# A four-layer attention kernel: dense outputs in the last layer, spaced background groups, and unread matmuls in thin tiles

## The chip, the core and the metric

The kernel runs on one core of a Trainium2 chip. The metric is the device time of one execution in microseconds (us). Before the change it is 2328.76 us, the median of 3 runs (2326.96 to 2332.97). Engine names in the profile: PE is TensorE's matmuls and PEld its weight loads, DVE is VectorE, ACT is ScalarE, POOL is GpSimd and SP is the engine that issues most transfers. A line such as L1284 is a line of the kernel's source.

## What is computed

Four layers on x of 2048 x 640 in bf16. Each normalizes x, projects it to queries, keys and values for 32 heads of 20, attends, and projects back. Layers 0 and 2 look at a window of 256 keys, layers 1 and 3 at all 2048.

```python
def layer(x, wqkv, wo, window):            # cut and merged from the reference
    h = layernorm(x)                       # no scale, no bias
    q, k, v = split_heads(h @ wqkv)        # 32 heads, 20 wide
    s = einsum("bhqd,bhkd->bhqk", q, k) * 20 ** -0.5
    if window: s = where(0 <= i - j < 256, s, -1e9)
    o = einsum("bhqk,bhkd->bhqd", softmax(s), v)
    return x + merge_heads(o) @ wo

x = layer(x, A_wqkv, A_wo, True)           # layer 0
x = layer(x, B_wqkv, B_wo, False)          # layer 1
x = layer(x, A_wqkv, A_wo, True)           # layer 2
x = layer(x, B_wqkv, B_wo, False)          # layer 3
```

## The kernel before

Work is cut into units: one layer l, one chunk c of 512 queries, one group g of 4 heads. A unit's scores are banks of 128 keys x 512 queries for one head. The main loop goes tile by tile: up to three banks of scores (two buffers, banks 0 to 2 and 3 to 5 of the 8 accumulator banks), one exponential over them on ACT, then the product with the values, two tiles behind. Bank 7 collects that product. All other work (normalizing, projections, outputs, the division by the softmax sum) is *background*: generators that a small scheduler advances between the scores of one tile and those of the next. For these, bank 6 is left, and bank 5 too in the early part of the program ("early"), when every second tile has only two banks.

The scheduler is Python that runs while the program is built, so all of it is fixed in the program. Each tile brings `rate` of credit, and a step of a task costs about its time on TensorE in units of 1 us. A task that yields "hold" is in the middle of an accumulation and goes on whatever the credit is; so a group of matmuls is never split by another task.

```python
def pump(credit, most):
    state["credit"] = min(state["credit"] + credit, most)
    while True:
        t = choose(state["credit"] <= 0.0)     # the held task; else a tail; else, unless blocked, the first of todo
        if t is None: break
        state["credit"] -= advance(t)

def drop_m(b):                                  # a background bank is given back
    mseq[0] += 1
    mfree[b] = (state["tick"] + (not state["early"]), mseq[0])
```

`advance` also counts *heat*: a step's cost divided by 0.22, weighted with 0.15 for tails and 0.7 for the normalization. After the background work of a tile, `keep_clock` adds matmuls that nobody reads until the tile's heat and what was carried over reach `least`, which is 1.76 for a full tile (1.0 early on) and 0 from the units of layer 3 with c > 0 on:

```python
def cool():
    return state["heat"] + state["carry"] < state["least"]

def unread(b):
    nc.tensor.matmul(ps[:, b, :], lhsT=ident[:], rhs=masks[:, 0, :], start=True, stop=True)   # L620
    state["heat"] += 1.0

def keep_clock():
    while cool():
        t = choose(False)
        if t is not None and state["credit"] > -0.5:
            state["credit"] -= advance(t)
            continue
        b = min(mfree, key=mfree.get)
        if mfree[b][0] > state["tick"]:
            break                               # no background bank is free in this tile
        unread(b)
    spare = state["heat"] + state["carry"] - state["least"]
    state["carry"] = min(max(spare, 0.0), 3.0)
    state["heat"] = 0.0
```

Each finished unit starts a *tail* of three steps, which need a background bank each: the softmax sums to a small matrix, its transpose, and the factors spread over the heads; the last line multiplies and stores into `on[:, g, :]`. There the 4 heads of a group lie on partitions 0, 32, 64 and 96, with 20 of each 32 rows used, so the output projection goes over 8 groups of 128 rows:

```python
def t_out(l, c):                                # [...] waits
    for qb in range(4):
        for i in range(2):
            mb = yield from take_m()
            yp = ps[:, mb, 0:HD]
            g0 = G - 2 if last else 0           # last: layer 3, chunk 3; its groups 0 to 5 were done by t_before_last
            for g in range(g0, G):
                nc.tensor.matmul(yp, lhsT=on[:, g, qb * P : (qb + 1) * P],      # L541
                                 rhs=wop[:, g, i * HD : (i + 1) * HD], ...)
                if g < G - 1:
                    yield ("hold", 0.14)
            # [...] add to x on VectorE, give the bank back
            yield ("pe", 0.14)
```

The loop that ties it together:

```python
def rate(t):
    if t >= len(tiles):                         # layer 3, c > 0
        return 0.9
    # [...] 1.2 before layer 1 is woven in; then what the open tasks need, at most 1.0 or 0.9

# for each tile t:
    sp = ps[:, 0:3, :] if t % 2 == 0 else ps[:, 3:7, :]
    # scores: nc.tensor.matmul(sp[:, i, ...], lhsT=u.k(kc, j), rhs=u.q(j, q0, qn), ...)   L1253
    # exponentials: nc.scalar.activation(out=pt[...], in_=sp[...], func=Exp)              L1284
    load_ahead()
    r = rate(t)
    pump(r, r + 0.1)
    keep_clock()
    # values: nc.tensor.matmul(op[32 * j : ...], lhsT=u.v(kc, j), rhs=pg[...], ...)       L1317
```

In layer 3 with c > 0 a tile may take four banks (the last of them bank 6) when no tail and no task is runnable. For the last keys of some units, VectorE computes the exponential instead of ACT (scores at L880, values at L1326).

Of the kernel before, what the change touches and what calls it, by code (L numbers as in the profile page):

```python
# [12 lines left out]
ALU = mybir.AluOpType  # L13
ACT = mybir.ActivationFunctionType

P = 128
# [3 lines left out]
DH = 20  # L20
NT = S // P
KD = D // P
G = 8
C = 512
NC = S // C
EPS = 1e-5
SCALE = DH ** -0.5
HD = D // 2
# [21 lines left out]
def kernel(  # L50
# [75 lines left out]
        nc.sync.dma_start(out=x_sb[:, 4 * c : 4 * c + 4, :], in_=xin[:, 4 * c : 4 * c + 4, :])  # L126
    nc.sync.dma_start(out=wv_sb[1][:], in_=wq_view[1][:, :, 2 * D : 3 * D])

    def load_wop(w):
        v = wo_in[w].rearrange("(g j e) f -> j e g f", g=G, j=4)  # L130
        for j in range(4):
            nc.sync.dma_start(out=wop[32 * j : 32 * j + DH, :, :], in_=v[j])
# [41 lines left out]
    ready = set()  # L174
    todo = []
    tails = []
    state = {"tick": 0, "held": None, "credit": 0.0, "early": True, "act": True, "unit": 0, "heat": 0.0, "carry": 0.0, "least": 0.0}

    class Task:

# [59 lines left out]

    def pump(credit, most):
        state["credit"] = min(state["credit"] + credit, most)
        while True:
            t = choose(state["credit"] <= 0.0)
            if t is None:
                break
            state["credit"] -= advance(t)


    mfree = {5: (0, 0), 6: (0, 1)}  # L250
# [278 lines left out]
    def t_out(l, c):  # L529
        on = ons[l, c]  # L530
        last = (l, c) == (3, NC - 1)
        while last and "before_last" not in ready:
            yield ("wait", 1)
        assert out_seq[out_n[0]] == l % 2
        for qb in range(4):
            for i in range(2):
                mb = yield from take_m()
                yp = ps[:, mb, 0:HD]
                g0 = G - 2 if last else 0
                for g in range(g0, G):  # L540
                    nc.tensor.matmul(  # L541
                        yp, lhsT=on[:, g, qb * P : (qb + 1) * P],
                        rhs=wop[:, g, i * HD : (i + 1) * HD],
                        start=(g == g0), stop=(g == G - 1),
                    )
                    if g < G - 1:
                        yield ("hold", 0.14)
                xv = x_sb[:, 4 * c + qb, i * HD : (i + 1) * HD]
                had = part_o["t"][:, 2 * qb + i, 0:HD] if last else xv
                nc.vector.tensor_tensor(out=xv, in0=had, in1=yp, op=ALU.add)  # L550
                drop_m(mb)
                yield ("pe", 0.14)
            if l < 3:
                stats(l + 1, c, qb)
            else:
                nc.sync.dma_start(out=xout[:, 4 * c + qb, :], in_=x_sb[:, 4 * c + qb, :])
        ons.pop((l, c))
        ready.add(("out", l, c))
        ready.add(("x", l + 1, c))
        n = out_n[0] = out_n[0] + 1  # L560
        if n < len(out_seq) and out_seq[n] != out_seq[n - 1]:
            load_wop(out_seq[n])

    def t_before_last():

        on = ons[3, NC - 1]
        for qb in range(4):
            for i in range(2):
                mb = yield from take_m()
                yp = ps[:, mb, 0:HD]  # L570
                for g in range(G - 2):
                    nc.tensor.matmul(
                        yp, lhsT=on[:, g, qb * P : (qb + 1) * P],
                        rhs=wop[:, g, i * HD : (i + 1) * HD],
                        start=(g == 0), stop=(g == G - 3),
                    )
                    if g < G - 3:
                        yield ("hold", 0.14)
                xv = x_sb[:, 4 * (NC - 1) + qb, i * HD : (i + 1) * HD]
                nc.vector.tensor_tensor(  # L580
                    out=part_o["t"][:, 2 * qb + i, 0:HD], in0=xv, in1=yp, op=ALU.add
                )
                drop_m(mb)
                yield ("pe", 0.14)
        ready.add("before_last")
# [27 lines left out]

    def cool():

        return state["heat"] + state["carry"] < state["least"]

    def unread(b):

        nc.tensor.matmul(  # L620
            ps[:, b, :], lhsT=ident[:], rhs=masks[:, 0, :], start=True, stop=True
        )
        state["heat"] += 1.0
# [8 lines left out]
# [5 lines that stand above are left out]
                state["credit"] -= advance(t)  # L637
                continue
            b = min(mfree, key=mfree.get)
            if mfree[b][0] > state["tick"]:  # L640
                break
            unread(b)
        spare = state["heat"] + state["carry"] - state["least"]
        state["carry"] = min(max(spare, 0.0), 3.0)
        state["heat"] = 0.0
# [360 lines left out]
    def t_tail(l, c, g, on, oT):  # L1006
        def fill(count):

            for n in range(count * ((l, c, g) == (3, NC - 1, G - 1))):
                nc.tensor.matmul(  # L1010
                    ps[:, 0, :], lhsT=ident[:], rhs=masks[:, 0, :], start=True, stop=True
                )

        yield ("wait", 2)
        fill(2)
        mb = yield from take_m()
        warm_bank(mb)
        zp = ps[:, mb, 0:16]
        for qb in range(4):
            nc.tensor.matmul(  # L1020
                zp[:, 4 * qb : 4 * qb + 4], lhsT=oT[:, qb * P : (qb + 1) * P],
                rhs=sel4[:], start=True, stop=True,
            )
        rz = rzp.tile([P, 16], F32, name="rz", tag="rz")
        nc.vector.reciprocal(out=rz[:], in_=zp)  # L1025
        drop_m(mb)

        hl = rzp.tile([P, 2, 16], BF16, name="hl", tag="hl")
        nc.vector.tensor_copy(out=hl[:, 0, :], in_=rz[:])
        nc.vector.tensor_tensor(out=hl[:, 1, :], in0=rz[:], in1=hl[:, 0, :], op=ALU.subtract)  # L1030
        yield ("pe", 0.25)
        fill(3)
        yield ("wait", 2)
        mb = yield from take_m()
        warm_bank(mb)
        rp = ps[0:32, mb, :].bitcast(BF16)[:, 0:P]
        nc.tensor.transpose(out=rp, in_=hl[:].rearrange("p n r -> p (n r)"), identity=ident[:])
        rT = rzp.tile([32, P], BF16, name="rT", tag="rT")
        nc.vector.tensor_copy(out=rT[:], in_=rp)  # L1039
        drop_m(mb)  # L1040
        yield ("pe", 0.1)
        fill(1)
        yield ("wait", 2 if state["tick"] < last_tick[0] else 1)
        mb = yield from take_m()
        warm_bank(mb)
        zb = ps[:, mb, :]
        for qb in range(4):
            nc.tensor.matmul(  # L1048
                zb[:, qb * P : (qb + 1) * P], lhsT=spread4[:, qb, :], rhs=rT[:],
                start=True, stop=True,  # L1050
            )
        nc.vector.tensor_tensor(out=on[:, g, :], in0=oT[:], in1=zb, op=ALU.mult)  # L1052
        drop_m(mb)
        yield ("pe", 0.3)
        fill(3)
        ready.add(("tail", l, c, g))
        if (l, c, g) == (3, NC - 1, G - 3):
            push("before_last", t_before_last(), 0, 8.0)
        if g == G - 1:
            need = first_use(l + 1, c, 0) if l < 3 else len(units) + c  # L1060
            push(("out", l, c), t_out(l, c), need, 9.0)
            if l < 3:
                push_layer(l + 1, c)
    def t_zeros():

        z = ka_all[:, G : G + 4, :].rearrange("p a b -> p (a b)")
        yield ("wait", 4)
        for n in range(2):
            nc.gpsimd.dma_start(
                out=wop[:, 4 * n : 4 * n + 3, :].rearrange("p g f -> p (g f)"), in_=z[:, 0 : 3 * D]  # L1070
            )
            nc.gpsimd.dma_start(out=wop[:, 4 * n + 3, :], in_=z[:, 0:D])
            yield ("wait", 1)
        load_wop(0)
        for t in (*kts, *qts):
            nc.gpsimd.dma_start(out=t[:], in_=z[:, 0 : t.shape[1]])
            yield ("wait", 1)
        ready.add("kts")
# [67 lines left out]
    with tc.manual_schedule():  # L1146
# [49 lines left out]
        def rate(t):  # L1196

            if t >= len(tiles):
                return 0.9
            u = tiles[t][0][0]  # L1200
            if index[u.l, u.c, u.g, u.part] < woven:
                return 1.2
# [16 lines left out]
        while ended is None or t < ended + 8:  # L1219
# [3 lines left out]
            if t < len(tiles) or banks:  # L1223
# [23 lines left out]
                if n_b == 4:  # L1247
                    mseq[0] += 1
                    mfree[6] = (state["tick"] + 2, mseq[0])
                for n in range(2):  # L1250
                    for i, (u, j, m, b0, subs, first, last, end) in enumerate(cur):
                        for kc, q0, qn, col in subs[n : n + 1]:
# [37 lines left out]
                    pts.append((t, pt, i, b))  # L1290
                warmth = 1.76 if state["unit"] >= woven else 1.0
                state["least"] = warmth * n_b / 3 if state["unit"] < index[3, 1, 0, None] else 0.0
                load_ahead()
                r = rate(t)
                pump(r, r + 0.1)
# [98 lines left out]
```

## Time and profile before

| | |
|---|---|
| median of 3 runs | 2328.76 us |
| profiled execution, span | 2334.1 us |
| busy: ACT / PE / DVE | 2177.3 / 2019.9 / 1465.6 us |
| mean granted TensorE clock | 0.852 of full |
| unread matmuls (L620) | 788 |
| output matmuls (L541, and 48 for the first part of the last chunk) | 976 |

The page gives the busy time of each engine and its share of the span, then the span in 40 slices with the busy share in tenths, and the clock that TensorE was granted, also in tenths. The groups that follow it are one line of the source each: the operation, output and input by the program's names, how often, total busy time and mean duration, and the idle time of the engine just before them with what ended it. A wait of one engine for another costs time only if that engine is the one that sets the pace of its stage. So the busy shares have to be read stage by stage.

### The profile page before, as it was taken

The page shows a single profiled execution, that of the slowest core. Times are in us where ns is not written, and L with a number is a line of the kernel's source. Part 1 is how long each engine was busy: PE and PEld are TensorE (multiplying, and loading weights), DVE is VectorE, ACT ScalarE, POOL GpSimd, SP SyncE. Part 2 cuts the span into 40 slices and gives each one's busy share as a digit, 9 for nine tenths or more (in the row PEclk, how much of TensorE's full clock was granted, in tenths as well). Part 3 has the DMA queues.
Part 4 walks back from the last instruction along what each step waited for, and adds up shares of the span by engine and source line. Part 5 has one row for each costly group of instructions (what it writes and reads, how often), then busy time and mean ns, then how long its engine had stood idle before and what let it go on. Part 6 is the DMA issues. An engine that isn't in the chain of part 4 may idle for free.

```text
span 2334.1 us, 40627 instructions
## 1 busy us (share of the span) xinstructions
PE 2019.9 (87%) x15793; PEld 725.3 (31%) x15793; DVE 1465.6 (63%) x2726; ACT 2177.3 (93%) x1751; POOL 273.7 (12%) x445
## 2 busy tenths in 40 slices
PE   8899999988899888888988898898878888888887
PEld 3344333333323332233322333342322122222222
DVE  6677776426646666666666544452677777777772
ACT  6788889999999998999899899999999999999997
POOL 4332321201100012000120013001000000000000
PEclk9999999999989999999999999999855565556556
DMA  6232322322200123102230023112200010011100
GB/s 189 82 88 79 100 75 64 83 64 65 83 19 27 46 69 95 48 14 55 75 103 25 18 84 107 39 27 78 64 29 27 27 38 27 27 38 37 29 14 12
DMA packets 84881, 132.57 MB, mean 57 GB/s; under 512 B 19760, under 2 KB 60080, under 8 KB 84688
## 3 DMA queue, kind: packets, MB, share of 16 engines
q1 hardware_dynamic: 65472, 76.80, 11.9%
q0 software_dynamic: 19216, 53.17, 7.9%
q8 instruction: 124, 2.03, 0.4%
q14 instruction: 69, 0.57, 0.1%
HBM read 98.70 MB, written 27.79 MB: 54 GB/s over the span
## 4 chain that ended last, share of the span: by engine, by line
ACT 41%; PE 28%; issue 14%; DVE 12%; DMA 1%; POOL 0%; SPq 0%; ACTq 0%; DVEq 0%; POOLq 0%
ACT pt L1284 40%; PE ps L1253 7%; PE ps L354 5%; PE ps L541 4%; PE ps L1317 4%; DVE pt L1353 3%; PE ps L455 3%; PE ps L620 2%; DVE st L304 1%; DVE on L1052 1%; ACT ka L1284 1%; DVE raw_o L887 1%; DVE oT L839 1%; PE ps L419 1%; DVE raw_o L897 1%
## 5 line engine op out<-in xcount | busy, mean ns | idle before, releaser
L1284 ACT ACTIVATE pt<-ps 128x1536 bf16<-128x1536 f32 (+2 forms) x1641 | 2100.2, 1502 | 114.8 <-PE ps L1253 107.0
L1253 PE MATMUL ps<-qt,kt 32*128 32x512 bf16 x4008 | 642.1, 456 | 192.8 <-ACT pt L1284 160.9
L1317 PE MATMUL ps<-pt,vt 128*21 128x512 bf16 x3860 | 466.9, 456 | 0.3 <-ACT pt L1284 0.3
L1253 PEld LDWEIGHTS <-kt 32*128 32x128 bf16 x4008 | 190.4, 94 | 610.8 <-issue 589.7
L1353 DVE TENSOR_TENSOR pt<-pt,masks 128x1024 bf16<-128x1024 bf16 (+5 forms) x403 | 238.0, 624 | 127.3 <-ACT pt L1284 126.8
L620 PE MATMUL ps<-masks,ident 128*128 128x512 bf16 x788 | 270.6, 396 | 28.3 <-DVE rT L1039 11.9
L354 PE MATMUL ps<-xnT,wqk 128*128 128x512 bf16 x830 | 220.2, 390 | 14.2 <-DVE on L1052 3.7
L1317 PEld LDWEIGHTS <-vt 128*21 128x21 bf16 x3960 | 100.0, 90 | 319.8 <-issue 310.6
L304 DVE CAST st<-ps 128x512 bf16<-128x512 f32 x128 | 88.4, 690 | 159.9 <-PE ps L354 159.7
L541 PE MATMUL ps<-wop,on 128*128 128x320 bf16 x976 | 167.6, 315 | 5.5 <-DVE x_sb L550 2.3
L1253 PE MATMUL ps<-qa,ka 32*128 32x384 bf16 (+2 forms) x1408 | 117.6, 277 | 30.6 <-ACT pt L1284 25.8
L887 DVE TENSOR_SCALAR xnT<-ps 128x512 int32<-128x512 f32 x88 | 60.8, 690 | 106.6 <-PE ps L880 106.2
L1052 DVE TENSOR_TENSOR on<-oT,ps 128x512 bf16<-128x512 bf16 x128 | 87.3, 682 | 59.9 <-PE ps L1048 57.3
L839 DVE CAST oT<-ps 128x512 bf16<-128x512 f32 x112 | 76.7, 685 | 73.4 <-PE ps L1317 49.1
L550 DVE TENSOR_TENSOR x_sb<-x_sb,ps 128x320 bf16<-128x320 bf16 x120 | 57.9, 482 | 100.3 <-PE ps L541 100.0
L455 PE MATMUL ps<-wv,xnT 128*128 128x320 bf16 x640 | 108.6, 302 | 10.4 <-DVE rz L1025 3.8
L541 PEld LDWEIGHTS <-on 128*128 128x128 bf16 x976 | 90.5, 101 | 71.6 <-issue 37.3
L354 PEld LDWEIGHTS <-wqk 128*128 128x128 bf16 x830 | 71.0, 98 | 110.4 <-issue 52.2
L620 PEld LDWEIGHTS <-ident 128*128 128x128 bf16 x788 | 59.3, 97 | 130.5 <-issue 128.6
L388 POOL TENSOR_SCALAR rstd<-mv 128x4 f32<-128x4 f32 x15 | 4.9, 328 | 794.1 <-DVE mv L375 794.1
L1317 PE MATMUL ps<-pt,va 128*21 128x384 bf16 (+2 forms) x1408 | 79.5, 283 | 6.9 <-DVE pt L1353 5.5
L1253 PEld LDWEIGHTS <-ka 32*128 32x128 bf16 x1408 | 44.3, 92 | 98.2 <-issue 89.8
(107 smaller groups left out, 1794.4 us busy)
## 6 DMA issues: line engine op xcount, KB each, us to landing
vt<-v_d SPq DMA_DIRECT2D x48, 336.0 KB
kt<-k_d SPq DMA_DIRECT2D x192, 80.0 KB
wqk<-in_B_wqkv_dram POOLq DMA_DIRECT2D x80, 160.0 KB, 3.9
wqk<-in_A_wqkv_dram POOLq DMA_DIRECT2D x70, 160.0 KB, 3.5
k_d<-st POOLq DMA_DIRECT2D x75, 128.0 KB, 2.2
q_d<-st POOLq DMA_DIRECT2D x75, 128.0 KB, 2.2
qt<-q_d SPq DMA_DIRECT2D x384, 20.0 KB
v_d<-vs POOLq DMA_DIRECT2D x16, 336.0 KB, 3.1
```

What stands on the lines that cost most here:

```text
L304: nc.vector.tensor_copy(out=out_, in_=in_)
L354: nc.tensor.matmul(pq, lhsT=wt[:, dc, :], rhs=xt[:, dc, :], start=(dc == 0), stop=(dc == KD - 1),)
L455: nc.tensor.matmul(pv, lhsT=xt[:, dc, i * P : (i + 1) * P], rhs=wv_sb[l % 2][:, dc, h * HD : (h + 1) * HD], start=(dc == 0), stop=(dc == K ...
L541: nc.tensor.matmul(yp, lhsT=on[:, g, qb * P : (qb + 1) * P], rhs=wop[:, g, i * HD : (i + 1) * HD], start=(g == g0), stop=(g == G - 1),)
L620: nc.tensor.matmul(ps[:, b, :], lhsT=ident[:], rhs=masks[:, 0, :], start=True, stop=True)
L839: nc.vector.tensor_copy(out=oT[:], in_=op)
L887: V.tensor_scalar(out=xi.bitcast(I32)[:, i * C : (i + 1) * C], in0=side["psum"], scalar1=SCALE * LOG2E * E23, scalar2=127.0 * E23, op0=ALU ...
L1052: nc.vector.tensor_tensor(out=on[:, g, :], in0=oT[:], in1=zb, op=ALU.mult)
L1253: nc.tensor.matmul(sp[:, i, col * P : (col + qn) * P], lhsT=u.k(kc, j), rhs=u.q(j, q0, qn), start=True, stop=True,)
L1284: nc.scalar.activation(out=pt[:, i:k, b0 * P :], in_=sp[:, i:k, b0 * P :], func=ACT.Exp, scale=SCALE,)
L1317: nc.tensor.matmul(op[32 * j : 32 * j + VW, q0 * P : (q0 + qn) * P], lhsT=u.v(kc, j), rhs=pg[:, i, col * P : (col + qn) * P], start=(first ...
L1353: nc.vector.tensor_tensor(out=pt_[:, i:k, b0 * P :], in0=pt_[:, i:k, b0 * P :], in1=mv_, op=ALU.mult,)
```

## The change

Three things are changed together.

*Spacing.* After the first step of a background task in a tile, a further task starts only when the credit left is over 0.6. Held tasks and tails are not affected.

*Dense outputs of the final layer.* In layer 3, a tail stores its group into a staging slot (5, 6 or 7 of `on`), and small transfers move each head's 20 rows to their place in 640 dense rows: five blocks of 128. The output weights are loaded in the same order, so a group of the projection takes 5 matmuls in place of 8. The last two groups of the last chunk keep the old layout; the first part of that chunk takes 4 in place of 6. The credit in layer 3 with c > 0 falls from 0.9 to 0.45 a tile.

*Unread matmuls in poor tiles.* From the units of layer 1 with c > 0 until `least` is 0, a tile counts as cool, too, while its own heat is under 0.9. Where no background bank is free, `keep_clock` no longer stops: it owes the matmul, and what is owed is issued into the first score bank of the next tile, ahead of its scores, which overwrite it.

```diff
 def pump(credit, most):
     state["credit"] = min(state["credit"] + credit, most)
+    floor = 0.0
     while True:
-        t = choose(state["credit"] <= 0.0)
+        t = choose(state["credit"] <= floor)
         if t is None:
             break
         state["credit"] -= advance(t)
+        if t not in tails:
+            floor = 0.6
```

```diff
+    def packed(l, c):
+        return l > 2
 # t_out
+        dense = packed(l, c) and not last
+        a, b = (0, KD) if dense else (G - 2 if last else 0, G)
-                for g in range(g0, G):
+                for g in range(a, b):
 # t_before_last (first part of the last chunk)
-                for g in range(G - 2):
+                for b in range(4):
+                    n = min(P, (G - 2) * 80 - b * P)
 # [...] operands on[0:n, b, ...] and wop[0:n, b, ...]
 # t_tail
-        nc.vector.tensor_tensor(out=on[:, g, :], in0=oT[:], in1=zb, op=ALU.mult)
+        end = (l, c) == (3, NC - 1) and g >= G - 2
+        spread = packed(l, c) and not end
+        nu = on[:, 5 + g % 3 if spread else g, :]
+        nc.vector.tensor_tensor(out=nu, in0=oT[:], in1=zb, op=ALU.mult)
 # [...]
+        if spread:
+            yield ("wait", 2)
+            for j in range(4):
+                r, a = (4 * g + j) * DH, 0
+                while a < DH:
+                    b, o = divmod(r + a, P)
+                    n = min(DH - a, P - o)
+                    nc.sync.dma_start(
+                        out=on[o : o + n, b, :], in_=nu[32 * j + a : 32 * j + a + n, :]
+                    )
+                    a += n
+            if g == G - 1 or (l, c, g) == (3, NC - 1, G - 3):
+                yield ("wait", 3)
 # rate
-                return 0.9
+                return 0.45
 # [...] load_wop(w, dense): the weights in dense order for layer 3, and the old order of the last two groups beside them
```

```diff
 def cool():
+        if state["least"] > 0.0 and state["heat"] < state["floor"]:
+            return True
         return state["heat"] + state["carry"] < state["least"]
 # keep_clock
             b = min(mfree, key=mfree.get)
-            if mfree[b][0] > state["tick"]:
+            if state["early"] and mfree[b][0] > state["tick"]:
                 break
-            unread(b)
+            if mfree[b][0] > state["tick"] - (0 if state["early"] else 0):
+                state["owed"] += 1
+                state["heat"] += 1.0
+            else:
+                unread(b)
 # main loop, ahead of a tile's scores
+                while state["owed"]:
+                    state["owed"] -= 1
+                    nc.tensor.matmul(
+                        sp[:, 0, :], lhsT=ident[:], rhs=masks[:, 0, :], start=True, stop=True
+                    )
 # main loop, after the exponentials
+                state["floor"] = 0.9 if state["unit"] >= index[1, 1, 0, None] else 0.0
```

More of the change, by code (lines that the diff above doesn't have):

```diff
@@ L127, with load_wop @@
     nc.sync.dma_start(out=wv_sb[1][:], in_=wq_view[1][:, :, 2 * D : 3 * D])
-    def load_wop(w):
+    def packed(l, c):
+        return l > 2
+    def load_wop(w, dense):
+        if dense:
+            nc.sync.dma_start(out=wop[:, 0:KD, :], in_=wo_in[w].rearrange("(b p) f -> p b f", p=P))
+            if w and out_n[0] == 12:
+                v = wo_in[w].rearrange("(g j e) f -> j e g f", g=G, j=4)
+                for j in range(4):
+                    nc.sync.dma_start(
+                        out=wop[32 * j : 32 * j + DH, G - 2 : G, :], in_=v[j][:, G - 2 : G, :]
+                    )
+            return
         v = wo_in[w].rearrange("(g j e) f -> j e g f", g=G, j=4)
@@ L176 @@
     tails = []
-    state = {"tick": 0, "held": None, "credit": 0.0, "early": True, "act": True, "unit": 0, "heat": 0.0, "carry": 0.0, "least": 0.0}
+    state = {"tick": 0, "held": None, "credit": 0.0, "early": True, "act": True, "unit": 0, "heat": 0.0, "carry": 0.0, "least": 0.0, "floor": 0.0, "owed": 0}
     class Task:
@@ L538, in t_out @@
                 yp = ps[:, mb, 0:HD]
-                g0 = G - 2 if last else 0
-                for g in range(g0, G):
+                for g in range(a, b):
                     nc.tensor.matmul(
@@ L543, in t_out @@
                         rhs=wop[:, g, i * HD : (i + 1) * HD],
-                        start=(g == g0), stop=(g == G - 1),
+                        start=(g == a), stop=(g == b - 1),
                     )
-                    if g < G - 1:
+                    if g < b - 1:
                         yield ("hold", 0.14)
@@ L560, in t_out @@
         n = out_n[0] = out_n[0] + 1
-        if n < len(out_seq) and out_seq[n] != out_seq[n - 1]:
-            load_wop(out_seq[n])
+        if n < len(out_seq) and (n == 12 or out_seq[n] != out_seq[n - 1]):
+            load_wop(out_seq[n], n >= 12)
     def t_before_last():
@@ L570, in t_before_last @@
                 yp = ps[:, mb, 0:HD]
-                for g in range(G - 2):
+                for b in range(4):
+                    n = min(P, (G - 2) * 80 - b * P)
                     nc.tensor.matmul(
-                        yp, lhsT=on[:, g, qb * P : (qb + 1) * P],
-                        rhs=wop[:, g, i * HD : (i + 1) * HD],
-                        start=(g == 0), stop=(g == G - 3),
+                        yp, lhsT=on[0:n, b, qb * P : (qb + 1) * P],
+                        rhs=wop[0:n, b, i * HD : (i + 1) * HD],
+                        start=(b == 0), stop=(b == 3),
                     )
-                    if g < G - 3:
+                    if b < 3:
                         yield ("hold", 0.14)
@@ L1055, in t_tail @@
         fill(3)
+        if spread:
+            yield ("wait", 2)
+            for j in range(4):
+                r, a = (4 * g + j) * DH, 0
+                while a < DH:
+                    b, o = divmod(r + a, P)
+                    n = min(DH - a, P - o)
+                    nc.sync.dma_start(
+                        out=on[o : o + n, b, :], in_=nu[32 * j + a : 32 * j + a + n, :]
[3 more added lines that the diff above has]
+                yield ("wait", 3)
         ready.add(("tail", l, c, g))
@@ L1073, in t_zeros @@
             yield ("wait", 1)
-        load_wop(0)
+        load_wop(0, False)
         for t in (*kts, *qts):
@@ L1249 @@
                     mfree[6] = (state["tick"] + 2, mseq[0])
+                while state["owed"]:
+                    state["owed"] -= 1
+                    nc.tensor.matmul(
+                        sp[:, 0, :], lhsT=ident[:], rhs=masks[:, 0, :], start=True, stop=True
+                    )
                 for n in range(2):
```

## The prediction

> **What bounds the kernel now.** I read four views in this order: the page's busy shares and slices, the costliest groups, the busy time by stretches of the span, and the order of TensorE's instructions inside two bad stretches. First the page:
>
> ```profile
> PE 2019.9 (87%) x15793; PEld 725.3 (31%) x15793; DVE 1465.6 (63%) x2726; ACT 2177.3 (93%) x1751; POOL 273.7 (12%) x445
> ...
> ACT  6788889999999998999899899999999999999997
> ...
> PEclk9999999999989999999999999999855565556556
> ...
> L1284 ACT ACTIVATE pt<-ps 128x1536 bf16<-128x1536 f32 (+2 forms) x1641 | 2100.2, 1502 | 114.8 <-PE ps L1253 107.0
> ...
> L620 PE MATMUL ps<-masks,ident 128*128 128x512 bf16 x788 | 270.6, 396 | 28.3 <-DVE rT L1039 11.9
> ```
>
> ACT, which does the exponentials, is busy 93% of the span. Its idle time, 2334.1 - 2177.3 = 156.8 us, is all that a change which leaves the exponentials alone can win, and 107.0 us of it is waiting for the score matmuls (L1253). TensorE's granted clock is near full for three quarters of the span and near half in the last quarter. L620 is the unread matmul that the kernel issues to keep the clock up. Now by stage:
>
> ```profile
> 0.00:300.00 300.00, 273.48 (x2401) 118.08 (x2401) 213.56 (x502) 238.76 (x272) 101.93 (x184) 0.96 0.37 108
> 300.00:535.00 235.00, 213.78 (x1788) 83.34 (x1789) 119.70 (x263) 218.62 (x183) 37.19 (x55) 0.99 0.26 72
> 535.00:1640.00 1105.00, 957.75 (x7962) 361.91 (x7961) 641.16 (x1233) 1056.85 (x816) 134.60 (x206) 0.97 0.21 56
> 1640.00:2300.00 660.00, 549.90 (x3513) 154.42 (x3513) 484.53 (x714) 642.00 (x470) 0.00 (x0) 0.57 0.10 31
> ```
>
> After the stretch and its length come the busy times of PE, PEld, DVE, ACT and POOL, then the clock. ACT's idle time is 61.2 us up to 300, 16.4 up to 535, 48.2 up to 1640, 18.0 up to 2300, and 13.0 in the last 34 us (the final tail, not touched). I put the borders where the program changes: near 535 the units of layer 1 with c > 0 begin (inferred: the first matmul with a DVE-made tile is at 560), and the last unread matmul outside the end is at 1649, so layer 3 with c > 0 begins about 1640.
>
> In stretches of 20 us between 535 and 1640, the ones below a full clock (560 to 620, 660 to 700, 840, 900 to 960, 1120, 1300 to 1340, 1360) hold 28.3 us of the 48.2. One of them, on TensorE's side:
>
> ```profile
> 1308.34 0.39 PE L1253 MATMUL ps<-qt,kt 32*128 32x512 bf16 x3
> 1309.74 0.38 PE L620 MATMUL ps<-masks,ident 128*128 128x512 bf16 x1 [1.01 <-DVE rT L1039]
> ...
> 1313.44 0.61 PE L1253 MATMUL ps<-qt,kt 32*128 32x512 bf16 x3
> ...
> 1317.64 2.31 PE L541 MATMUL ps<-wop,on 128*128 128x320 bf16 x8
> ```
>
> TensorE stands 1.01 us because bank 6 is still with VectorE; 3 us later the three scores take 0.61 instead of 0.39 us, and the output group that follows takes 2.31 us where a tile lasts about 1.34. In the last stage, with the clock at half, the same group opens each burst:
>
> ```profile
> 1889.71 2.29 PE L541 MATMUL ps<-wop,on 128*128 128x320 bf16 x8 [0.44 <-DVE on L1052]
> ...
> 1892.74 1.26 PE L541 MATMUL ps<-wop,on 128*128 128x320 bf16 x8
> ```
>
> **What the skill says.** The Trainium skill, "TensorE: Matmul & The Clock Gate", Part 1, says that activity releases the throttle, that there are two states (half and full), and that the window is about 3.4 us. This trace agrees: 0.50 and 1.00 in long stretches, 0.61 against 0.39 us for the same scores, and a drop some 3 us after the stall. The same page, Part 3, says that matmuls on different row groups run concurrently: three scores together take 0.39 us here, so a tile's own work is short and the background group is what can make it late. "Perfetto Trace Analysis", "Identifying the Most-Contended Engine", warns that TensorE's busy share is no measure of its headroom, and that occupancy serves for ScalarE: hence I count ACT's idle time, not PE's 87%. "DMA: Bandwidth & Descriptors", "Anatomy of one DMA", puts about 2 us of fixed cost on a DMA; the trace has 2.2 us from issue to landing for the 128 KB stores of k and q, and no SBUF to SBUF copy of 20 KB to compare with.
>
> **Part 1, dense outputs at half pace (from 1640).** A group of eight 128x320 matmuls becomes five. Three chunks have 8 groups each: 3 x 8 x 3 = 72 matmuls fewer; the first part of the last chunk has 4 in place of 6: 16 fewer. Scaled from the two durations above, a group of five costs 2.29 x 5/8 = 1.43 us cold and 1.26 x 5/8 = 0.79 warm. A warm tile then needs 0.33 (scores, start to start) + 0.33 (values) + 0.79 = 1.45 us, against 1.85 from one score group to the next now (1892.41 to 1894.26) and 1.35 for the exponential ((1766.05 - 1740.44) / 19). At 0.45 credit a tile and 0.70 a group, about two tiles in three carry a group, so on average TensorE keeps up once warm. Cold, the tile needs 0.54 + 0.54 + 1.43 = 2.5 us, still more than 1.35, and the burst may stay cold for longer because it is thinner. ACT's idle time lies almost wholly in the four bursts: 4.3 us (1660 to 1700), 5.1 (1880 to 1920), 4.7 (2100 to 2140), 3.4 (2260 to 2300), 17.5 in all. My choice: each keeps 1 to 2 us, so 6.5 remain, **-11 us**. What it adds: 32 heads + 4 cuts at block borders = 36 small copies a chunk (27 in the last), 135 in all, on a queue whose issues take about 0.33 us each; they have a wait of 2 or 3 tiles and feed only the output, so nothing on the path. Longer tails and longer output tasks leave fewer chances for the four-bank exponential (25 now). That one takes 1.76 us start to start for four banks, 0.440 a bank against 1.348 / 3 = 0.449: losing all of them would cost 25 x 4 x 0.009 = 0.9 us, **+1**.
>
> **Part 2, unread matmuls in poor tiles (535 to 1640).** Today the filling stops when bank 6 is taken. Such tiles are above all those in which a tail has the bank: 64 tails with 3 steps, 192 tiles. The change owes the matmul and issues it into a score bank ahead of the next tile's scores, where the only wait is the one the scores have anyhow; and each tile now needs 0.9 of heat of its own, whatever was carried over. I expect 1 to 1.5 for each of these tiles and some tens more in the tile after a full group: 200 to 350 added to 788. Gain: of the 28.3 us lost at a reduced clock I give it half, -14; not more, because the stall that begins a drop is a wait for VectorE, which stays. Cost: an unread matmul adds about 0.22 us before the scores. Where there is slack (TensorE waits for ACT there) it is free; in tiles with a background group it is not. A third of them, some 90, at 0.22 is 20 us of TensorE time, of which a quarter may reach ACT through the two score buffers: +5. Sum **-9**.
>
> **Part 3, a second group only above 0.6 credit (mostly before 535).** Once only bank 6 is left (after about 500), a bank is given back one tile later, so two groups cannot share a tile and the rule rarely acts. Before, at 1.2 a tile (at most 1.3), a projection of 1.1 leaves 0.2, so its follower is put off: 1.1 a tile in place of 1.2. A value group of 0.7 leaves 0.6, which is not over 0.6: one instead of 1.7 a tile. TensorE is busy 273.5 of the first 300 us and the work is the same, only later, so most of it comes back as forced work at the units' starts. I give it **-2**, with 6 either way.
>
> Sum: -11 + 1 - 9 - 2 = -21, so 2328.76 - 21 = **2308 us**.
>
> **Rivals.** (a) The owed matmuls crowd heavy tiles: for it, ACT already loses about 2 us in each of 860, 880, 1160 and 1420 at a clock of 1.00, so those stretches are bound by TensorE's amount of work; if all 20 us reach ACT and the drops stay, part 2 is +15 and the time about 2332. (b) The later background work of part 3 piles up at the units' starts: for it, the first 300 us leave TensorE 26 us of slack; against it, ACT is idle 61 us there anyway. It would add up to 10 to 15 us: about 2320. (c) All goes well: drops vanish (-25), bursts cost nothing (-17), part 3 gives -8: about 2280.
>
> **Range and chances.** The parts are independent and each about 6 to 10 us uncertain, so some 14 us for the sum, a little more for what I have not seen: 2289 to 2328 eight times in ten. Faster by over 2% means under 2282, which needs rival (c): 0.07. Slower by over 2% needs 47 us lost with ACT's work unchanged: 0.03. Within 2%: 0.90.
>
> **What would show it.** Right: L541 falls from 976 to 904 matmuls and the other output line from 48 to 32; ACT's idle time in the four bursts falls to some 6 us; unread matmuls near 1050; fewer low-clock stretches between 535 and 1640 and idle time there near 39 us; little change before 535. Wrong: as many drops as before, or ACT's idle time at full clock up by over 5 us (rival a), or more than 66 us idle before 300 (rival b).

## The result, and the profile after

The changed kernel takes **2297.95 us** (median, 2295.7 to 2300.23) against 2330.69 for the kernel before in the same measurement: a ratio of 0.9861, with a 95% interval from 0.9843 to 0.988. That is 32 us less, by 28 to 37. The prediction had 21 us less and a range that holds the measured time. But two of its three terms were wrong by more than the whole error of the sum, and in part they cancelled. So the total says little about the mechanism, and the parts have to be measured apart.

The same lines of the page as before, now of the changed kernel (line numbers have moved):

```profile
PE 1981.5 (86%) x15618; PEld 709.1 (31%) x15772; DVE 1468.5 (64%) x2736; ACT 2172.7 (95%) x1742; POOL 273.2 (12%) x445
...
ACT  6789899999999999999899999999999999999997
...
PEclk9899999999999999999999999999765565556556
...
L1329 ACT ACTIVATE pt<-ps 128x1536 bf16<-128x1536 f32 (+2 forms) x1645 | 2105.8, 1473 | 84.0 <-PE ps L1298 71.0
...
L640 PE MATMUL ps<-masks,ident 128*128 128x512 bf16 x655 | 228.5, 385 | 35.2 <-DVE rT L1063 9.2
```

ACT's work is what it was (2172.7 against 2177.3 us). Its wait for the scores fell from 107.0 to 71.0 us. The count of L640 is too low, since some matmul records are missing: its weight loads number 743, and 112 more belong to the line that issues what is owed. So unread matmuls rose from 788 to 855, not to 1050. They fell by 48 before 482 us and rose by 115 after it.

To see where the time went, fixed times won't do, because everything moves. I used marks that both programs have: VectorE's first copy of a part of layer 1 to `raw_o` (layer 1 is woven in), its first addition there, the first and the last `oT` that is made from `raw_o`, and the end. Stretches between them, first before and then after (columns: stretch and length, PE, PEld, DVE, ACT, POOL, clock, share and rate of transfers):

```profile
0.00:179.40 179.40, 158.87 (x1379) 70.90 (x1379) 124.10 (x315) 135.49 (x185) 65.60 (x128) 0.95 0.40 121
179.40:303.10 123.70, 117.32 (x1053) 48.26 (x1051) 90.76 (x193) 106.34 (x91) 38.61 (x59) 0.97 0.32 90
303.10:482.40 179.30, 166.03 (x1403) 65.23 (x1400) 100.97 (x211) 162.95 (x141) 34.91 (x52) 0.99 0.27 74
482.40:1653.80 1171.40, 1013.28 (x8410) 383.45 (x8410) 662.92 (x1291) 1123.25 (x866) 134.60 (x206) 0.97 0.21 57
1653.80:2334.00 680.20, 564.45 (x3554) 157.48 (x3553) 486.87 (x719) 649.31 (x474) 0.00 (x0) 0.56 0.10 29
```

```profile
0.00:175.50 175.50, 150.57 (x1315) 66.96 (x1334) 124.84 (x318) 130.66 (x175) 54.68 (x113) 0.93 0.37 109
175.50:292.20 116.70, 109.36 (x1026) 45.33 (x1037) 87.78 (x188) 105.71 (x91) 37.18 (x58) 1.00 0.32 92
292.20:463.60 171.40, 159.62 (x1392) 64.73 (x1404) 106.18 (x221) 164.19 (x141) 44.29 (x65) 1.00 0.34 90
463.60:1625.40 1161.80, 1013.75 (x8427) 384.22 (x8532) 663.82 (x1293) 1123.96 (x865) 137.09 (x211) 1.00 0.22 59
1625.40:2294.00 668.60, 548.24 (x3465) 147.81 (x3465) 485.88 (x719) 648.15 (x475) 0.00 (x0) 0.56 0.11 33
```

The second column shows it: the three early stretches (together 482.4 us) lost 18.8 us, the middle 9.6 and the last 11.6. The profiled executions differ by 40 us and the medians by 32: the profile of the kernel before is of an execution of 2335.83 us, 5 us above its median. Where two kernels below have the same early or middle program, their profiles differ by 2 to 4 us there. So a stretch is good for a few us, and the timed ratios decide.

### The profile page after: what moved, and what is told of

The parts are those of the page before. It is cut to its first block, busy times and chain, and to the rows that moved or that the text cites. A ratio compares the mean times of both kernels' runs of the same rounds, so it can differ in the third digit from the quotient of the medians.

```text
span 2293.9 us, 40624 instructions
## 1 busy us (share of the span) xinstructions
PE 1981.5 (86%) x15618; PEld 709.1 (31%) x15772; DVE 1468.5 (64%) x2736; ACT 2172.7 (95%) x1742; POOL 273.2 (12%) x445
## 4 chain that ended last, share of the span: by engine, by line
ACT 41%; PE 30%; issue 14%; DVE 13%; DMA 1%; POOL 0%; SPq 0%; ACTq 0%; another core or an unknown queue 0%; DVEq 0%; POOLq 0%
ACT pt L1329 40%; PE ps L1298 7%; PE ps L370 6%; PE ps L1363 5%; PE ps L558 4%; PE ps L471 3%; DVE pt L1399 3%; PE ps L640 2%; DVE st L320 1%; DVE on L1079 1%; DVE raw_o L911 1%; DVE oT L863 1%; ACT ka L1329 1%; PE ps L1292 1%; DVE x_sb L567 1%
## 5 line engine op out<-in xcount | busy, mean ns | idle before, releaser
L1298 PEld LDWEIGHTS <-kt 32*128 32x128 bf16 x4008 | 182.5, 93 | 582.9 <-issue 562.6
L640 PE MATMUL ps<-masks,ident 128*128 128x512 bf16 x655 | 228.5, 385 | 35.2 <-DVE rT L1063 9.2
L370 PE MATMUL ps<-xnT,wqk 128*128 128x512 bf16 x765 | 209.0, 384 | 19.1 <-issue 3.2
L558 PE MATMUL ps<-wop,on 128*128 128x320 bf16 x904 | 161.0, 315 | 8.5 <-DVE x_sb L567 4.0
L558 PEld LDWEIGHTS <-on 128*128 128x128 bf16 x904 | 81.5, 101 | 74.7 <-issue 46.6
L640 PEld LDWEIGHTS <-ident 128*128 128x128 bf16 x743 | 57.9, 96 | 128.0 <-issue 126.2
```

The source lines that it names most:

```text
L370: nc.tensor.matmul(pq, lhsT=wt[:, dc, :], rhs=xt[:, dc, :], start=(dc == 0), stop=(dc == KD - 1),)
L558: nc.tensor.matmul(yp, lhsT=on[:, g, qb * P : (qb + 1) * P], rhs=wop[:, g, i * HD : (i + 1) * HD], start=(g == a), stop=(g == b - 1),)
L1298: nc.tensor.matmul(sp[:, i, col * P : (col + qn) * P], lhsT=u.k(kc, j), rhs=u.q(j, q0, qn), start=True, stop=True,)
```

## The experiments

All are compared with the kernel before on the same chip. "us less" is (1 - ratio) times the kernel before, with the interval's half width.

**One part alone.** First the spacing rule:

```diff
# kernel before, pump
+        floor = 0.0
-            t = choose(state["credit"] <= 0.0)
+            t = choose(state["credit"] <= floor)
             state["credit"] -= advance(t)
+            if t not in tails:
+                floor = 0.6
```

> The kernel before with the spacing rule alone. Theory A (the three parts act in their own stages and add up; the first 480 us of the changed kernel were 19 us shorter, and only this rule acts there): 10 to 20 us faster than before, nearly all of it before the mark at 482 us, and the rest of the program as long as before (within 4 us). Rival B (the rule only moves work, as the prediction had it): within 5 us of before. Rival C (the rule also spaces work in the middle, and part of the middle's gain is its own): over 20 us faster, with the stretch from 482 to 1654 us shortened by 5 or more and its stretches of low clock fewer.

Measured: 2307.26 us, ratio 0.9897 (0.9879 to 0.9916): **24 us less**, 4 either way. The early stretches are as short as in the changed kernel, and the middle is, too:

```profile
173.80:290.60 116.80, 109.33 (x1026) 45.31 (x1037) 87.72 (x188) 105.66 (x91) 37.14 (x58) 1.00 0.32 92
290.60:461.80 171.20, 159.65 (x1392) 64.84 (x1404) 106.19 (x222) 164.16 (x141) 44.28 (x65) 1.00 0.33 90
461.80:1624.60 1162.80, 986.78 (x8281) 381.28 (x8386) 664.39 (x1294) 1120.98 (x865) 138.71 (x211) 0.98 0.21 58
```

So the middle's 9.6 us can't be credited to the added unread matmuls: 8.6 of them are here without any. (Two kernels with the old middle, the dense outputs alone at either pace, have 1168.4 and 1169.6 us there, so some 2 to 3 us of both figures belong to the one profile of the kernel before.) Theory A's 20 us are exceeded. The pieces of 10 us below full clock in the middle are 17 as before, so rival C is right in the length and wrong in the reason. The prediction's view of this part (rival B) falls.

The unread matmuls alone:

```diff
# kernel before: cool(), keep_clock(), the loop ahead of the scores, and state["floor"], as in the change
+        if state["least"] > 0.0 and state["heat"] < state["floor"]:
+            return True
...
+            if mfree[b][0] > state["tick"]:
+                state["owed"] += 1
```

> The kernel before with the unread matmuls in poor tiles alone. Theory A: 7 to 12 us faster, all between 482 and 1654 us, with the clock there near 1.00 in place of 0.97; some 110 matmuls owed to the score bank. Rival B (the loss at low clock comes back as idle time at full clock, so it is worth little by itself): within 4 us of before, with the clock near 1.00 all the same. Rival C (the middle's gain belongs to the spacing): within 4 us of before and the clock still 0.97.

Measured: 2334.64 us, ratio 1.0021 (1.001 to 1.0032): **5 us more**. Its middle is as long as before in the profile, though the clock rose:

```profile
479.70:1651.10 1171.40, 1022.73 (x8443) 387.28 (x8551) 661.78 (x1291) 1126.44 (x866) 132.44 (x206) 0.99 0.21 57
```

That is rival B, and a little worse.

The dense outputs at half pace alone:

```diff
# the changed kernel
-        floor = 0.0            # [...] spacing taken out
-                state["owed"] += 1      # [...] unread matmuls in poor tiles taken out
```

> The kernel before with the dense outputs at half pace alone. Theory A: 8 to 13 us faster, all after the mark at 1654 us (680 us there before, 668 in the changed kernel). Rival B (the half at which the clock stands in this stage depends on what came before, so part of it belongs to the other parts): under 6 us faster.

Measured: 2319.31 us, ratio 0.995 (0.9932 to 0.9967): **12 us less**, 4 either way, as theory A had it. And the changed kernel without the spacing:

```diff
# the changed kernel, pump
-            t = choose(state["credit"] <= floor)
+            t = choose(state["credit"] <= 0.0)
```

> The changed kernel without the spacing rule. Theory A (parts add up): 14 to 22 us faster than before, that is 10 to 20 us slower than the changed kernel, with the first 480 us as long as before. Rival (the parts overlap): within 6 us of the changed kernel, or over 24 us faster than before.

Measured: 2323.08 us, ratio 0.9973 (0.9958 to 0.9987): 6 us less, about what 12 less and 5 more make. It is less than theory A had, since that counted on a gain from the unread matmuls. The parts do add up: 24 + 12 - 5 = 31 us, against 32 for all three.

**Where the spacing acts.** Only while two background banks are open:

```diff
-            if t not in tails:
+            if t not in tails and state["early"]:
                 floor = 0.6
```

> The kernel before with the spacing rule acting only while two background banks are open (up to about 480 us). Theory A (what the rule wins, it wins there, and the middle is shorter because it starts with other work left over): 20 to 26 us faster, the first mark near 462 us and the middle stretch near 1163 us as with the whole rule. Theory B (the rule acts in the middle as well): 14 to 20 us faster, the first mark near 462 us and the middle stretch near 1171 us.

Measured: 2311.55 us, ratio 0.9917 (0.9901 to 0.9933), 19 us less; the mark at 482 us moved to 463.5, and the middle stretch is 1165.1 us. The time is theory B's and the middle nearer to theory A's. Only with one bank:

```diff
-            if t not in tails:
+            if t not in tails and not state["early"]:
                 floor = 0.6
```

> The kernel before with the spacing rule acting only after the second background bank is closed (from about 480 us on). Theory A (in that part a bank comes back one tile later, so the rule has nothing to put off): within 3 us of before. Theory B: 4 to 10 us faster, all in the middle stretch, 1171 us before.

Measured: 2330.81 us, ratio 1.0001 (0.9987 to 1.0015): nothing, 3 us either way, though its profile had a middle of 1163.7 us. So nearly all of the gain is won before 480 us. Whether the rule adds something in the middle beside it (24 against 19 us) lies within the intervals, and stays open.

**Pace or spacing?** The rule also slows the work. So, without it, less credit in the first stage:

```diff
             if index[u.l, u.c, u.g, u.part] < woven:
-                return 1.2
+                return 1.05
```

> The kernel before with the credit of the first stage at 1.05 a tile in place of 1.2 and no spacing rule. Theory P (what counts is the pace: work of the first 300 us is put off to where unread matmuls stood, which are then not issued): 12 to 20 us faster, the mark at 482 us moved to 462 to 468, some 40 unread matmuls fewer before it. Theory S (what counts is that two groups no longer stand between two tiles' scores): within 6 us of before, though the unread matmuls fall by as many.

Measured: 2322.55 us, ratio 0.9967 (0.9956 to 0.9978), 8 us less: between the two theories. The mark moved to 473.3 us, and the unread matmuls before it fell by 15 only, not by 40. The rule in the first stage only, and in the two after it only:

```diff
-            if t not in tails:
+            if t not in tails and state["unit"] < woven:                          # first run
+            if t not in tails and state["early"] and state["unit"] >= woven:      # second run
                 floor = 0.6
```

> The kernel before with the spacing rule acting only until layer 1 is woven in (mark at 179 us). Theory P (pace: what counts is that work of the first stage is put off to where unread matmuls stand): most of the early gain, 12 us or more, with the unread matmuls between 303 and 482 us at half of their 87. Theory S (what counts is that groups no longer follow each other within a tile, in each stage for itself): only the first stage is shorter, by 3 to 5 us, and the two after it stay near 122 and 180 us.

> The kernel before with the spacing rule acting only from there until the second background bank is closed (179 to 482 us). Theory P: under 6 us faster, because no work is put off from the first stage. Theory S: 12 to 16 us faster, with these two stages near 117 and 171 us though the first is as long as before.

Measured: 2321.31 us, ratio 0.9959 (0.9945 to 0.9973), 10 us less in the first; 2311.02 us, ratio 0.9906 (0.9892 to 0.992), **22 us less** in the second, as much as the whole rule. The first run's stretches are 176.4, 118.5 and 177.4 us: the two later ones are shorter too, by 5.2 and 1.9 us, though the rule does not act there. So putting work off has a worth of its own, less than theory P had. The second run is theory S in kind and above it in size. As 10 and 22 us do not add up to the whole rule's 24, the two gains overlap. The second's stretches:

```profile
0.00:178.30 178.30, 156.39 (x1356) 70.25 (x1374) 123.61 (x313) 135.37 (x185) 65.10 (x128) 0.95 0.40 121
178.30:290.40 112.10, 104.88 (x1010) 43.91 (x1017) 85.95 (x188) 104.62 (x91) 29.94 (x47) 1.00 0.30 84
290.40:463.00 172.60, 159.58 (x1377) 63.90 (x1390) 103.41 (x218) 164.29 (x141) 41.28 (x61) 0.99 0.31 83
```

The first stage is as long as before; the next two lost 11.6 and 6.7 us. What was put off from the first stage is thus not needed for the gain. The same piece of work in both kernels shows the spacing itself. The normalization of a chunk, before:

```profile
436.78 0.39 PE L1253 MATMUL ps<-qt,kt 32*128 32x512 bf16 x2
437.10 0.60 PE L620 MATMUL ps<-masks,ident 128*128 128x512 bf16 x2
437.70 0.45 PE L419 MATMUL ps<-ident,xn 128*128 128x128 bf16 x5
437.99 0.59 PE L620 MATMUL ps<-masks,ident 128*128 128x512 bf16 x2
438.42 0.44 PE L419 MATMUL ps<-ident,xn 128*128 128x128 bf16 x5
438.79 0.40 PE L1317 MATMUL ps<-pt,vt 128*21 128x512 bf16 x4
439.12 0.39 PE L1253 MATMUL ps<-qt,kt 32*128 32x512 bf16 x3
```

```profile
439.67 1.45 ACT L1284 ACTIVATE pt<-ps 128x1536 bf16<-128x1536 f32 x1 [0.95 <-PE ps L1253]
```

and with the rule in these stages:

```profile
424.91 0.39 PE L1256 MATMUL ps<-qt,kt 32*128 32x512 bf16 x3
425.23 0.60 PE L623 MATMUL ps<-masks,ident 128*128 128x512 bf16 x2
425.68 0.44 PE L422 MATMUL ps<-ident,xn 128*128 128x128 bf16 x5
426.05 0.40 PE L1320 MATMUL ps<-pt,vt 128*21 128x512 bf16 x4
426.38 0.39 PE L1256 MATMUL ps<-qt,kt 32*128 32x512 bf16 x2
```

```profile
420.11 7.80 ACT L1287 ACTIVATE pt<-ps 128x1024 bf16<-128x1024 f32 x7
```

Two groups of a row block (two unread matmuls and five transposes each) stood between two tiles' scores, which came 2.34 us after the last ones (436.78 to 439.12), and ACT stood 0.95 us. With one group a tile the scores come after 1.47 us, and ACT runs seven tiles without a gap.

Work is left out as well. Weight loads before the first `oT` from `raw_o`, by group (first, second and third stretch):

| | projections | unread | us before that mark |
|---|---|---|---|
| before | 210, 120, 100 | 27, 23, 87 | 482.4 |
| whole rule | 175, 110, 135 | 27, 19, 43 | 461.8 |
| rule in first stage | 180, 120, 130 | 27, 19, 72 | 472.3 |
| rule in the woven stages | 210, 85, 125 | 27, 19, 49 | 463.0 |
| slower pace | 190, 120, 120 | 25, 19, 78 | 473.3 |

Projections are the matmuls of L354, to queries and keys; the value projections (320), outputs (256) and transposes (140) before the mark are as many in all five kernels. With the whole rule 48 unread matmuls are not issued and 10 projection matmuls come later: at some 0.22 us apiece (1.25 us for a group of five, less the overlap at its end), an estimate of 58 x 0.22 = 13 us of TensorE's time, of the 20.6 us gained.

ACT's waits for the scores from 179 us to the mark (in all, times, longest), before and with the rule in the woven stages, fell by 19.7 us; these stages gained 18.3:

```profile
ACT pt L1284 <- PE ps L1253: 31.8, 48, 2.0
ACT pt L1287 <- PE ps L1256: 12.1, 26, 1.6
```

I sorted these waits by what TensorE issued between the two groups of scores ahead of each. Where two groups stood together, as in the normalization above, 8.3 us before; its transposes with the rule, one group a tile, 5.1. At the other tiles with one group, 19.3 before and 6.9 with the rule; at tiles with none, 4.2 and nothing. So the pair of groups shown above accounts directly for some 3 us only. Most of the gain lies at tiles with a single group. Whether they profit from the spread of the groups over the tiles, or from the unread matmuls left out (137 before, 95 with the rule in the woven stages), is not shown, since no run leaves those out without the rule. That the pace alone gives 8 us is measured.

**Without the unread matmuls.** Spacing and dense outputs together:

```diff
# the changed kernel: cool(), keep_clock() and the loop ahead of the scores as before the change
-        if state["least"] > 0.0 and state["heat"] < state["floor"]:
-            return True
...
-                state["owed"] += 1
```

> The changed kernel without the unread matmuls in poor tiles, that is spacing and dense outputs together. If the parts add up and that part alone costs 5 us: 34 to 37 us faster than before, near 2295 us, and 2 to 5 us faster than the changed kernel. If that part pays once the work is spaced: slower than the changed kernel by 2 to 8 us, near 2303 us.

Measured: 2295.19 us, ratio 0.9849 (0.9832 to 0.9867): 35 us less, about what 24 and 12 make. Against 0.9861 for the changed kernel the intervals overlap: whether it is faster is not settled, but the part brings nothing here either. Its middle and the changed kernel's, in pieces of 10 us:

| | pieces below full clock | ACT idle in them | ACT idle at full clock |
|---|---|---|---|
| before | 17 | 23.7 us | 24.4 us |
| unread matmuls alone | 8 | 9.9 | 35.1 |
| spacing and dense outputs | 17 | 20.3 | 19.7 |
| changed kernel (all three) | 3 | 3.0 | 34.9 |
| owed matmuls without the demand (next run) | 7 | 10.8 | 30.7 |

The part does what it is for, and what it saves at a low clock returns at full clock: 17 us saved and 15 added from the third row to the fourth. That is not the same idle time counted under another clock: at the places of the 17 slow pieces of the kernel before, ACT's idle time falls from 23.7 to 10.9 us with the unread matmuls alone, and everywhere else it rises from 24.4 to 34.1.

Which half of it costs? The owed matmuls without the demand on each tile:

```diff
# kernel before: keep_clock() and the loop ahead of the scores as in the change; cool() untouched
+            if mfree[b][0] > state["tick"]:
+                state["owed"] += 1
```

> The kernel before with the owed matmuls, but without the 0.9 of heat that each tile must have of its own. Unread matmuls in all alone cost 5 us. If the cost lies in the matmuls put ahead of the scores: still 3 to 8 us slower, with the low-clock stretches as few. If it lies in the demand on each tile, which also pulls background work into tiles that had none: within 2 us of before or faster by up to 8.

Measured: 2332.64 us, ratio 1.0001 (0.9989 to 1.0013). It has 728 unread matmuls in the middle, 115 of them owed; with the demand there are 792, 110 of them owed; before 651. So the 5 us seem to go with the demand of 0.9 a tile and not with the place ahead of the scores; the two intervals overlap a little (1.001 to 1.0032 and 0.9989 to 1.0013), so this is not settled.

**Fewer matmuls or half the pace?**

```diff
# dense outputs alone, rate
-                return 0.45
+                return 0.9
```

> The kernel before with the dense outputs at the old credit of 0.9 in the last layer. The dense outputs at half pace are 12 us faster. If the fewer matmuls bring the gain: 8 to 12 us faster here as well. If the pace brings a good part of it: 3 to 7 us faster, with ACT idle 2 to 3 us in each of the three bursts of outputs.

Measured: 2320.67 us, ratio 0.9954 (0.9939 to 0.9969), 11 us less against 12: the five matmuls bring the gain. The pace shows no effect that can be told from none.

## Why the prediction was right, and where it was not

*Dense outputs (-11 + 1).* Right: -12, 4 either way. A burst in the changed kernel:

```profile
1869.71 1.51 PE L558 MATMUL ps<-wop,on 128*128 128x320 bf16 x5
...
1872.23 0.95 PE L558 MATMUL ps<-wop,on 128*128 128x320 bf16 x5
...
1873.99 0.85 PE L558 MATMUL ps<-wop,on 128*128 128x320 bf16 x5
```

1.51 cold and 0.85 warm, where 1.43 and 0.79 were worked out. ACT is idle for 8.5 us in the four bursts (3.0, 2.3, 2.0 and 1.2) in place of 17.5; I had 6.5. Matmuls fell to 904 and 32 as counted. The four-bank exponentials fell from 25 to 22; the 1 us for them is too small to be seen. What the Trainium skill, "TensorE: Matmul & The Clock Gate", Part 1, says of a half clock was the right ground for this part: at that clock, 0.50, a group of eight took 2.29 us, longer than a tile of 1.35.

*Unread matmuls (-9).* Wrong in sign: +5, 3 either way. The gain was right in mechanism and size: at the places of low clock ACT's idle time fell by 12.8 us (23.7 to 10.9), and the prediction had 14. The failed term is the cost: "a third of them, some 90, at 0.22 is 20 us of TensorE time, of which a quarter may reach ACT". The added matmuls are fewer than the 200 to 350 expected, 141 (792 against 651 in the middle), and yet elsewhere ACT's idle time rose by 9.7 us in place of 5. ACT's own busy time in the middle rose as well, from 1123.25 to 1126.44 us, which the prediction did not have; why is open. These three sum to about nothing in the profiles, whose baseline is 5 us above its median; the timed runs say 5 us more. It was the prediction's own rival (a), at a smaller size.

*Spacing (-2).* Wrong in size: -24. The step that failed: "the work is the same, only later, so most of it comes back as forced work at the units' starts". It did not come back. Part of it filled tiles for which unread matmuls would have been issued (137 before the mark, 89 with the rule); with the projections put off, that is worth an estimated 13 us of TensorE's time. And how the groups stood between the scores counted beside the sum of work: with the rule from 179 us on, ACT waits for scores 12.1 us in place of 31.8, most of the difference at tiles with one group. I read 273.5 us busy of the first 300 as a full engine; the 50 matmuls that nobody reads up to 303 us are 18 us of it, and some stood in just the tiles whose scores came late. How the 24 us divide between less work and better spacing stays open. The other half of the step held: with one bank the rule did nothing.

*The total* came out near by luck in part: -10 stands against -12, but the other two terms, -9 and -2, against +5 and -24, the one 14 us too hopeful, the other 22 us not hopeful enough.

## What to carry to other kernels

Before a stage is called bound by an engine's amount of work, subtract from that amount what is issued only to fill it, and look at how the background work is spread over the pieces on the critical path: holding a tile to one group in two stages won 22 us here. Matmuls that keep a clock up can cost as much as they win, so count ACT's idle time at full clock and at low clock apart. And test the parts of a bundled change alone, even when the total came out as predicted.

## What was not expected of the hardware

In the last stage the half clock costs ACT nothing outside the bursts: from 1920 to 2080 us of the changed kernel ACT is busy all of the time at a clock of 0.50. A fuller clock in the middle, 1.00 in place of 0.98, bought no time either once the unread matmuls that kept it up were paid for (changed kernel against spacing and dense outputs: ratios 0.9861 and 0.9849).
